# Moving the last GLU weight conversions into the GLU's first pass, with another split order in the main slots

## The chip, the cores and the metric

The kernel runs on one core of a Trainium2 chip. The metric is the device time of one execution in microseconds (us). The kernel before takes 869.46 us (median of three runs, 868.57 to 869.98).

## The reference, cut to what matters

```python
state = f[:, :, t, :, None] * state + k_t (outer) v_t      # linear attention, 4 x 8 heads, 768 steps of 48
y[:, :, t] = q_t @ state
logits = x @ w_gate + modality_bias[modality_id]           # x: y as 3072 tokens of 384
e_idx = argmax(logits); gate_w = softmax(logits)[e_idx]    # one of 8 experts for each token
out[e] = gate_w * (relu(x @ w1[e]) @ w2[e])                # 384 -> 1024 -> 384
gate = 1 / (1 + exp(-(x @ w_gate)))                        # GLU: 384 -> 1536 -> 384
out = (gate * (x @ w_val)) @ w_out
```

The inputs of the GLU's weights reach the chip as 64-bit floats; every other large input is fp32, and the result is fp32.

## The kernel before, in words

**Stages.** Linear attention runs over 24 tiles of 128 tokens, 26 loop iterations with the ends of its pipeline, and ends at about 155 us. Two early expert tiles (`slot32`) follow, then half-size expert positions to about 223 us, then ten **main slots** p = 11 to 20 (`position`, which calls `slot`), up to about 409 us, and last the **GLU**: six passes `t` over 512 tokens each, with twelve steps `f` in a pass. A step is `glu_in` (gate and value projections of 128 columns) and, one step later, `glu_out`.

**Splits.** A matrix product of fp32 precision is made from three products of two rounded parts. `split` (L391 to L394) makes the parts of a weight piece: ScalarE (ACT) copies the piece into the high part, and VectorE (DVE) or GpSimd (POOL) subtracts that from the piece for the low part.

**Slots.** A main slot has ten places f0 to f9 in its row of products, and at each a table `hooks` says what else is issued there. In `position`, the tuple `at` names the places at which the four weight pieces x = 0, 2, 1, 3 of the next slot are split; x = 1 subtracts on POOL, the others on DVE. A split frees its `raw` buffer, and the load of the piece for the slot after goes out on the SP queue at once. At f7 the next slot's tokens are transposed (`transpose_x`, L408 to L411), and POOL issues the gathers of the tokens after them (L398). The ten hidden chunks h of a slot leave through ACT (`hh`, L667) and DVE (`hl`, L668).

**Conversions.** The GLU's weights are nine pieces of 128 x 1536 values in doubles, converted to fp32 half a piece at a time, so 18 conversions. One conversion is a load of 768 KB (`convert_load`), a mask on ACT (`convert_mask`, L849), two DVE operations (`convert_high`, L855 and L858), two more (`convert_low`, L866 and L869) and a store to the DRAM scratch `wd` (`convert_store`); pieces 3 and 7 stay in SBUF tiles `stage` instead. Four conversions stand in attention, at iterations `CONV`, two in the second `slot32`, seven in slots 12 to 18 at f0 and f1, and five more in the slots of `TWICE`, at f5 and f8. In slot 20 the three pieces of `LAST` (4, 5 and 8), by then in `wd`, are loaded into `raw` buffers, and in GLU steps 0 to 5 `split_last` splits a half of one in each step, with POOL's subtraction. Step 1 also splits piece 7 from `stage`, whole, with POOL's subtraction. Pieces 4 and 5 are wanted by `glu_in` at f = 8 of the first pass, piece 8 by `glu_out` at f = 8.

**The GLU's step.** In `glu_in` a gate tile and a value tile (PSUM, tag `gv`, three buffers) are filled by 18 products each. For each half (256 tokens) ACT makes the sigmoid of the gate (L1659), DVE multiplies it by the value (L1660), ACT copies the product to `gh` (L1661), and DVE subtracts for `gl` (L1662). With three buffers in turn, the value tile of step n takes the buffer that held the gate tile of step n - 1. The engines take their instructions in program order, and the hooks in the table `more` (one list for each step n) come behind the step's multiplications on DVE and copies on ACT:

```python
for n, (t, f, halves) in enumerate(seq):
    glu_in(t, f, halves, 256 if n < len(seq) - 1 else 128)
    for step in more.get(n, ()):
        step()
```

Of the kernel before, what the change touches and what calls it, by code (L numbers as in the profile page):

```python
# [14 lines left out]
I32 = mybir.dt.int32  # L15
# [22 lines left out]
NSLOT = NHALF + NSTAT  # L38
# [2 lines left out]
ORDER = (0, 2, 1, 3)  # L41
ROUTE = ((0, 4), (4, 4), (8, 4), (12, 4), (16, 2), (18, 4), (22, 2))
CUM = len(ROUTE) % 2
CONV = (3, 7, 11, 15)
GROUPED = 17
PUT = (9, 13, 17)
GROUP = (0, 6, 1, 2)
STAGED = (3, 7)
PADS = (320, 160, 352, 96)
LAST = ((4, 0), (5, 2), (8, 1))  # L50
TWICE = (13, 14, 16, 17, 18)
MIN_DECAY = 1e-18
MIN_LOGIT = -43.0
CAP = 1e36
# [8 lines left out]
def kernel(  # L63
# [16 lines left out]
    nc = tc.nc  # L80
# [309 lines left out]
    def split(dst, src, eng=None):  # L390

        hi, lo = dst
        nc.scalar.copy(out=hi, in_=src)
        (eng or nc.vector).tensor_tensor(out=lo, in0=src, in1=hi, op=ALU.subtract)  # L394
# [19 lines left out]
    tabs, hp = {}, {}  # L414
# [399 lines left out]
        return ys  # L814


    todo = [(j, half) for j in (0, 1, 6, 2, 3, 7, 4, 5, 8) for half in range(2)]
    loaded, done = [], []
    stage = {}

    def half_of(t, half):
        return t[:, half * 768:(half + 1) * 768]

    def convert_buffers():

        if "cv" in hp:
            cv = hp["cv"]
            return (
                cv.tile([P, 1536], I32, tag="cvr", name="cvr", bufs=2), cv.tile([P, 768], F32, tag="cvm", name="cvm", bufs=2),
                cv.tile([P, 768], I32, tag="cvt", name="cvt"),  # L830
            )
        n = len(todo) % 2 * 2
        return raw[n].bitcast(I32), raw[n + 1][:, 0:768], raw[n + 1][:, 768:1536].bitcast(I32)

    def convert_load():
        if not todo:
            return
        j, half = todo.pop(0)
        r, m, t = convert_buffers()
        if j in stage:  # L840
            m = half_of(stage[j], half)
        nc.sync.dma_start(out=r, in_=w_glu[j].bitcast(I32)[:, half * 1536:(half + 1) * 1536])
        loaded.append((j, half, r.rearrange("p (n o) -> p n o", o=2), m, t))
# [33 lines left out]
            j, half, m = done.pop(0)  # L877
            nc.sync.dma_start(out=half_of(wd[j], half), in_=m)

    def split_last(n, half):  # L880
        j, x = LAST[n]
        split([half_of(t, half) for t in glu[j]], half_of(raw[x], half), nc.gpsimd)


    hp["p"] = ctx.enter_context(tc.tile_pool(name="hp", bufs=2))
# [629 lines left out]
    def position(p, w, w_next):  # L1515
# [12 lines left out]
            each(hooks, f0=[lambda: part(w[2], 2, 1), lambda: load_group(p + 1, 2)], f1=lambda: split_group(p, 1, w), f2=lambda: split_group(p, 3, w))  # L1528
        if NSLOT - NSTAT < p < NSLOT - 2:
            each(hooks, f0=[convert_mask, convert_high], f1=[convert_low, convert_store, convert_load])  # L1530
        if p in TWICE:
            each(hooks, f5=[convert_mask, convert_high], f8=[convert_low, convert_store])
        if p + 1 in TWICE:
            each(hooks, f8=convert_load)
        if p >= NSLOT - NSTAT:
            at = ((2, 0), (3, 2), (4, 1), (6, 3))
            if p == NSLOT - NSTAT:
                at = ((4, 0), (5, 2), (7, 1), (9, 3))
            if p == NSLOT - 1:
                at = ((0, 0), (1, 2), (2, 1), (3, 3))  # L1540
            for f, x in at:
                each(hooks, **{f"f{f}": lambda x=x: split_group(p + 1, x, w_next, nc.gpsimd if x == 1 else None)})
        if p == NSLOT - 1:
            for f, (j, x) in enumerate(LAST):
                each(hooks, **{f"f{f}": lambda j=j, x=x: nc.sync.dma_start(out=raw[x], in_=wd[j])})
        if p == NSLOT - 2:
            each(hooks, f8=lambda: load_x2(0))
        if p == NSLOT - 1:
# [180 lines left out]
    for j, x in ((7, 2), (5, 3)):  # L1729
        glu[j] = alloc_w(*pools[(NSLOT + 1) % 2], x)  # L1730
    glu[8] = alloc_w(wc, "c", 0)
    more = {
        0: [lambda: split_last(0, 0), lambda: split_last(0, 1)],
        1: [lambda: scatter_y(tabs["dst"][:, NSLOT + 4]), lambda: split(glu[7], stage[7], nc.gpsimd)],
        2: [lambda: split_last(1, 0), lambda: load_x2(1)],
        3: [lambda: split_last(1, 1)],
        4: [lambda: split_last(2, 0)],
        5: [lambda: split_last(2, 1)],
    }
    psum.close()  # L1740
    ps_g = psum.enter_context(tc.tile_pool(name="ps_g", bufs=3, space=PSUM))
# [80 lines left out]
```

## Time and profile before

| what | before |
|---|---|
| median of the runs | 869.46 us |
| the profiled execution | 869.35 us |
| its span | 867.6 us |
| granted TensorE clock, mean | 0.993 |
| matmul engine (PE) busy | 843.4 us, 97% of the span |
| DVE busy | 481.2 us, 55% |
| ACT busy | 389.5 us, 45% |
| POOL busy | 251.1 us, 29% |
| main slots | 223.9 to 409 us |
| GLU | 409 us to the end |

The span is the stretch in which the engines work; the execution's time has 1.75 us around it. Busy shares are over the whole span: PE's 97% says that nearly all time passes beside matmuls, not that each of them runs at its shortest.

### The profile page before, as it was taken

Reading aid. Unit: us, or ns where it says so; the run is one execution under the profiler, and the core shown is the slowest. Engines: PE = TensorE matmul, PEld = TensorE weight load, DVE = VectorE, ACT = ScalarE, POOL = GpSimd, SP = SyncE. Lnnn points to the kernel's source line nnn. Section 1 sums busy time; section 2 is a strip of 40 time slices with the busy share of each in tenths; the row PEclk is TensorE's granted clock in tenths of the full one; section 3 lists DMA queues with packets and bytes.
Section 4 is the critical chain, followed back from the end, with each engine's and each line's share of the span. In section 5 each row is a group of like instructions: output and inputs, shape, how many; then the busy total and the mean of one; then the engine's idle time right before and its main releaser. Section 6 shows DMA issues by size and latency. Waiting matters only on the chain.

```text
span 867.6 us, 15306 instructions
## 1 busy us (share of the span) xinstructions
PE 843.4 (97%) x5802; PEld 762.0 (88%) x5802; DVE 481.2 (55%) x1036; ACT 389.5 (45%) x804; POOL 251.1 (29%) x321
## 2 busy tenths in 40 slices
PE   8999999999999999999999999999999999999995
PEld 6999988778999999999888888888888888888885
DVE  5788897576878979964435234334432523342221
ACT  5868664236766666656433322322232332232222
POOL 4755542125265646655620200020020011002002
PEclk9999999999999999999999999999999999999998
DMA  8677745757989889875111120021012002001000
GB/s 300 199 239 265 257 141 225 264 198 229 349 293 329 298 287 322 330 248 195 56 28 47 46 46 19 1 65 28 19 45 46 19 12 54 10 0 37 1 1 36
DMA packets 52273, 121.15 MB, mean 140 GB/s; under 512 B 21018, under 2 KB 33318, under 8 KB 52192
## 3 DMA queue, kind: packets, MB, share of 16 engines
q1 hardware_dynamic: 47200, 105.10, 36.1%
q0 software_dynamic: 4992, 15.00, 5.0%
q8 instruction: 47, 0.77, 0.4%
q14 instruction: 34, 0.28, 0.1%
HBM read 96.44 MB, written 20.11 MB: 134 GB/s over the span
## 4 chain that ended last, share of the span: by engine, by line
PE 68%; DVE 5%; issue 2%; ACT 1%; POOL 0%; DMA 0%; POOLq 0%; DVEq 0%; ACTq 0%
PE gv L1650 11%; PE gv L1651 11%; PE gv L1649 11%; PE y L740 8%; PE o L1674 6%; PE o L1672 6%; PE o L1673 6%; PE h L664 3%; PE h L661 3%; PE h L662 3%; DVE cvt L855 2%; DVE al L394 1%; DVE hl L668 1%; PE xT L408 0%; DVE bl L394 0%
## 5 line engine op out<-in xcount | busy, mean ns | idle before, releaser
L1660 DVE TENSOR_TENSOR sg<-sg,gv 128x256 f32<-128x256 f32 (+1 forms) x145 | 60.2, 415 | 209.4 <-PE gv L1651 209.4
L1661 ACT CAST gh<-sg 128x256 fp32r<-128x256 f32 (+1 forms) x145 | 58.7, 405 | 191.6 <-DVE sg L1660 191.6
L1680 POOL DMA_INDIRECT out_dram<-raw,tok x24 | 23.6, 984 | 375.6 <-ACT raw L1677 368.1
L1662 DVE TENSOR_TENSOR gl<-sg,gh 128x256 fp32r<-128x256 f32 (+1 forms) x145 | 64.3, 443 | 68.2 <-ACT gh L1661 68.2
L1659 ACT ACTIVATE sg<-gv 128x256 f32<-128x256 f32 (+1 forms) x145 | 55.2, 381 | 94.7 <-PE gv L1651 92.6
L398 POOL DMA_INDIRECT xg<-xd,ids x24 | 36.6, 1525 | 61.6 <-PE xT L408 37.2
L667 ACT ACTIVATE hh<-h 128x256 fp32r<-128x256 f32 x80 | 30.8, 386 | 42.5 <-PE h L664 41.5
L668 DVE SCALAR_TENSOR_TENSOR hl<-h,hh 128x256 fp32r<-128x256 f32 x80 | 33.4, 419 | 21.7 <-ACT hh L667 21.4
L950 POOL TENSOR_TENSOR qT<-kq,g 128x512 f32<-128x512 f32 x19 | 28.6, 1507 | 54.4 <-issue 34.5
L1651 PE MATMUL gv<-oddh,al 128*128 128x512 f32 (+1 forms) x120 | 44.3, 369 | 0.0
L1650 PE MATMUL gv<-oddl,ah 128*128 128x512 f32 (+1 forms) x120 | 44.3, 369 | 0.0
L1649 PE MATMUL gv<-oddh,ah 128*128 128x512 f32 (+1 forms) x120 | 44.1, 367 | 0.0
L1651 PE MATMUL gv<-oddh,bl 128*128 128x512 f32 x108 | 42.5, 394 | 0.0
L1651 PE MATMUL gv<-evenh,bl 128*128 128x512 f32 x108 | 42.5, 393 | 0.0
L1650 PE MATMUL gv<-oddl,bh 128*128 128x512 f32 x108 | 42.4, 393 | 0.0
L1650 PE MATMUL gv<-evenl,bh 128*128 128x512 f32 x108 | 42.4, 393 | 0.0
L1651 PE MATMUL gv<-evenh,al 128*128 128x512 f32 x108 | 42.3, 391 | 0.0
L1650 PE MATMUL gv<-evenl,ah 128*128 128x512 f32 x108 | 42.2, 391 | 0.0
L1649 PE MATMUL gv<-evenh,ah 128*128 128x512 f32 x108 | 42.0, 389 | 0.0
L1649 PE MATMUL gv<-evenh,bh 128*128 128x512 f32 x108 | 42.0, 389 | 0.0
L1649 PE MATMUL gv<-oddh,bh 128*128 128x512 f32 x108 | 42.0, 389 | 0.0
L980 DVE TENSOR_TENSOR am<-a,causal 128x512 f32<-128x512 f32 x48 | 31.7, 682 | 7.9 <-PE a L974 7.9
(365 smaller groups left out, 2490.3 us busy)
## 6 DMA issues: line engine op xcount, KB each, us to landing
raw<-in_w_dram SPq DMA_DIRECT2D x48, 768.0 KB, 6.0
kq<-in_att_kq_dram SPq DMA_DIRECT2D x24, 512.0 KB, 5.4
cvr<-in_w_glu_dram SPq DMA_DIRECT2D x14, 768.0 KB, 7.4
raw<-wd SPq DMA_DIRECT2D x7, 768.0 KB, 5.4
f<-in_att_fv_dram SPq DMA_DIRECT2D x24, 200.0 KB, 4.5
v<-in_att_fv_dram SPq DMA_DIRECT2D x24, 200.0 KB, 4.4
x<-yd SPq DMA_DIRECT2D x12, 386.0 KB, 3.5
xd<-rows SPq DMA_DIRECT2D x5, 772.0 KB, 5.2
```

What stands on the lines that cost most here:

```text
L668: nc.vector.scalar_tensor_tensor(out=hl, in0=ps, scalar=0.0, in1=hh, op0=ALU.max, op1=ALU.subtract)
L740: nc.tensor.matmul(out=ps, lhsT=lhs[:, ts], rhs=rhs[:, fs], start=(g == 0 and part == 0), stop=(g == 7 and part == 2))
L1649: nc.tensor.matmul(out=ps[:, ns], lhsT=hi[:, sl], rhs=xh[:, c, ns], start=(c == 0), stop=False)
L1650: nc.tensor.matmul(out=ps[:, ns], lhsT=hi[:, sl], rhs=xl[:, c, ns], start=False, stop=False)
L1651: nc.tensor.matmul(out=ps[:, ns], lhsT=lo[:, sl], rhs=xh[:, c, ns], start=False, stop=(c == 2))
L1659: nc.scalar.activation(out=sg[:, sl], in_=pss[0][:, to], func=AF.Sigmoid)
L1660: nc.vector.tensor_tensor(out=sg[:, sl], in0=sg[:, sl], in1=pss[1][:, to], op=ALU.mult)
L1661: nc.scalar.copy(out=gh[:, sl], in_=sg[:, sl])
L1662: nc.vector.tensor_tensor(out=gl[:, sl], in0=sg[:, sl], in1=gh[:, sl], op=ALU.subtract)
L1672: nc.tensor.matmul(out=ps, lhsT=gh[:, ts], rhs=hi[:, fs], start=(f == 0), stop=False)
L1673: nc.tensor.matmul(out=ps, lhsT=gh[:, ts], rhs=lo[:, fs], start=False, stop=False)
L1674: nc.tensor.matmul(out=ps, lhsT=gl[:, ts], rhs=hi[:, fs], start=False, stop=(f == 11))
```

## The change

Iteration 15 of attention no longer converts, `TWICE` is gone, and the six halves of pieces 4, 5 and 8 are no longer converted ahead. `load_last` brings their doubles into `raw` buffers (two of them in slot 20, one in step 0, two in step 2, one in step 4, into the `stage` tiles), and `convert_last` in GLU steps 0 to 5 converts one half and splits it, the subtraction on DVE. In the main slots the split of x = 3 moves from f6 to f7, behind the transposes; in slot 11 all four move one or two places ahead.

```diff
@@ -41,14 +41,13 @@
 ORDER = (0, 2, 1, 3)
 ROUTE = ((0, 4), (4, 4), (8, 4), (12, 4), (16, 2), (18, 4), (22, 2))
 CUM = len(ROUTE) % 2
-CONV = (3, 7, 11, 15)
+CONV = (3, 7, 11)
 GROUPED = 17
 PUT = (9, 13, 17)
 GROUP = (0, 6, 1, 2)
 STAGED = (3, 7)
 PADS = (320, 160, 352, 96)
-LAST = ((4, 0), (5, 2), (8, 1))
-TWICE = (13, 14, 16, 17, 18)
+LAST = tuple((j, half) for j in (4, 5, 8) for half in range(2))
 MIN_DECAY = 1e-18
 MIN_LOGIT = -43.0
 CAP = 1e36
@@ -814,7 +813,7 @@
         return ys
 
 
-    todo = [(j, half) for j in (0, 1, 6, 2, 3, 7, 4, 5, 8) for half in range(2)]
+    todo = [(j, half) for j in (0, 1, 6, 2, 3, 7) for half in range(2)]
     loaded, done = [], []
     stage = {}
 
@@ -835,8 +834,9 @@
     def convert_load():
         if not todo:
             return
-        j, half = todo.pop(0)
-        r, m, t = convert_buffers()
+        take_half(*todo.pop(0), *convert_buffers())
+
+    def take_half(j, half, r, m, t):
         if j in stage:
             m = half_of(stage[j], half)
         nc.sync.dma_start(out=r, in_=w_glu[j].bitcast(I32)[:, half * 1536:(half + 1) * 1536])
@@ -877,9 +877,16 @@
             j, half, m = done.pop(0)
             nc.sync.dma_start(out=half_of(wd[j], half), in_=m)
 
-    def split_last(n, half):
-        j, x = LAST[n]
-        split([half_of(t, half) for t in glu[j]], half_of(raw[x], half), nc.gpsimd)
+    def load_last(n):
+        a, b = (raw[0:2], raw[2:4], raw[0:2], [stage[j] for j in STAGED])[n if n < 4 else 2 + n % 2]
+        take_half(*LAST[n], a.bitcast(I32), b[:, 0:768], b[:, 768:1536].bitcast(I32))
+
+    def convert_last():
+        convert_mask()
+        convert_high()
+        convert_low()
+        j, half, m = done.pop(0)
+        split([half_of(t, half) for t in glu[j]], m)
 
 
     hp["p"] = ctx.enter_context(tc.tile_pool(name="hp", bufs=2))
@@ -1528,21 +1535,16 @@
             each(hooks, f0=[lambda: part(w[2], 2, 1), lambda: load_group(p + 1, 2)], f1=lambda: split_group(p, 1, w), f2=lambda: split_group(p, 3, w))
         if NSLOT - NSTAT < p < NSLOT - 2:
             each(hooks, f0=[convert_mask, convert_high], f1=[convert_low, convert_store, convert_load])
-        if p in TWICE:
-            each(hooks, f5=[convert_mask, convert_high], f8=[convert_low, convert_store])
-        if p + 1 in TWICE:
-            each(hooks, f8=convert_load)
         if p >= NSLOT - NSTAT:
-            at = ((2, 0), (3, 2), (4, 1), (6, 3))
+            at = ((2, 0), (3, 2), (4, 1), (7, 3))
             if p == NSLOT - NSTAT:
-                at = ((4, 0), (5, 2), (7, 1), (9, 3))
+                at = ((3, 0), (4, 2), (5, 1), (8, 3))
             if p == NSLOT - 1:
                 at = ((0, 0), (1, 2), (2, 1), (3, 3))
             for f, x in at:
                 each(hooks, **{f"f{f}": lambda x=x: split_group(p + 1, x, w_next, nc.gpsimd if x == 1 else None)})
         if p == NSLOT - 1:
-            for f, (j, x) in enumerate(LAST):
-                each(hooks, **{f"f{f}": lambda j=j, x=x: nc.sync.dma_start(out=raw[x], in_=wd[j])})
+            each(hooks, f4=lambda: load_last(0), f5=lambda: load_last(1))
         if p == NSLOT - 2:
             each(hooks, f8=lambda: load_x2(0))
         if p == NSLOT - 1:
@@ -1730,12 +1732,12 @@
         glu[j] = alloc_w(*pools[(NSLOT + 1) % 2], x)
     glu[8] = alloc_w(wc, "c", 0)
     more = {
-        0: [lambda: split_last(0, 0), lambda: split_last(0, 1)],
-        1: [lambda: scatter_y(tabs["dst"][:, NSLOT + 4]), lambda: split(glu[7], stage[7], nc.gpsimd)],
-        2: [lambda: split_last(1, 0), lambda: load_x2(1)],
-        3: [lambda: split_last(1, 1)],
-        4: [lambda: split_last(2, 0)],
-        5: [lambda: split_last(2, 1)],
+        0: [convert_last, lambda: load_last(2)],
+        1: [lambda: scatter_y(tabs["dst"][:, NSLOT + 4]), lambda: split(glu[7], stage[7], nc.gpsimd), convert_last],
+        2: [convert_last, lambda: load_x2(1), lambda: load_last(3), lambda: load_last(4)],
+        3: [convert_last],
+        4: [convert_last, lambda: load_last(5)],
+        5: [convert_last],
     }
     psum.close()
     ps_g = psum.enter_context(tc.tile_pool(name="ps_g", bufs=3, space=PSUM))
```

DVE in slot 13, one of those with a second conversion. `al_...<-raw_118`, `raw_120` and `raw_121` are the split subtractions of x = 0, 2 and 3, `xtl` the transposes' one. Before:

```order
L394 TENSOR_TENSOR al_4482<-raw_118,ah_4481 128x1536
L668 SCALAR_TENSOR_TENSOR hl<-h,hh 128x256
L394 TENSOR_TENSOR al_4486<-raw_120,ah_4485 128x1536
L668 SCALAR_TENSOR_TENSOR hl<-h,hh 128x256 x2
L855 TENSOR_SCALAR cvt<-cvr 128x768
L858 SCALAR_TENSOR_TENSOR cvt<-cvr,cvt 128x768
L668 SCALAR_TENSOR_TENSOR hl<-h,hh 128x256
L394 TENSOR_TENSOR al_4488<-raw_121,ah_4487 128x1536
L668 SCALAR_TENSOR_TENSOR hl<-h,hh 128x256
L411 TENSOR_TENSOR xtl<-xT,xth 128x3x128 x2
L866 SCALAR_TENSOR_TENSOR cvt<-cvr,cvt 128x768
L869 SCALAR_TENSOR_TENSOR stage_2943<-stage_2943,cvt 128x768
```

And changed (all lines of `split` and of the slots are one less there):

```order
L393 TENSOR_TENSOR al_4471<-raw_118,ah_4470 128x1536
L667 SCALAR_TENSOR_TENSOR hl<-h,hh 128x256
L393 TENSOR_TENSOR al_4475<-raw_120,ah_4474 128x1536
L667 SCALAR_TENSOR_TENSOR hl<-h,hh 128x256 x4
L410 TENSOR_TENSOR xtl<-xT,xth 128x3x128 x2
L393 TENSOR_TENSOR al_4477<-raw_121,ah_4476 128x1536
```

The four operations of the second conversion are gone from between the `hl`, and the subtraction of x = 3 stands behind the transposes.

POOL from the entry of slot 11 to its outputs; `al_...<-raw_119` is the split subtraction of x = 1. Before, and then changed:

```order
L641 COPY cur<-xc 128x4
L647 COPY xc<-xg 128x4
L398 DMA xg<-xd,ids 128x386 x2
L394 TENSOR_TENSOR al_3994<-raw_119,ah_3993 128x1536
L690 COPY ysb<-cur 128x2 x2
```

```order
L640 COPY cur<-xc 128x4
L393 TENSOR_TENSOR al_3987<-raw_119,ah_3986 128x1536
L646 COPY xc<-xg 128x4
L397 DMA xg<-xd,ids 128x386 x2
L689 COPY ysb<-cur 128x2 x2
```

The subtraction moved from behind the gathers to ahead of them and of the copy of `xc`.

DVE in GLU step 0 and at the start of step 1, changed. `sg` is the multiplication, `gl` the subtraction of a half, `raw_118` the doubles and `raw_119` the converted half:

```order
L1662 TENSOR_TENSOR sg<-sg,gv 128x256
L1664 TENSOR_TENSOR gl<-sg,gh 128x256
L1662 TENSOR_TENSOR sg<-sg,gv 128x256
L1664 TENSOR_TENSOR gl<-sg,gh 128x256
L855 TENSOR_SCALAR raw_119<-raw_118 128x768
L858 SCALAR_TENSOR_TENSOR raw_119<-raw_118,raw_119 128x768
L866 SCALAR_TENSOR_TENSOR raw_119<-raw_118,raw_119 128x768
L869 SCALAR_TENSOR_TENSOR raw_119<-raw_119 128x768
L393 TENSOR_TENSOR al_6310<-raw_119,ah_6309 128x768
L1662 TENSOR_TENSOR sg<-sg,gv 128x256
```

Before, the two `sg` and two `gl` of step 1 follow those of step 0 directly; now five operations stand between, and the same five in each of the steps 1 to 5. On ACT, step 1 now reads:

```order
L1663 CAST gh<-sg 128x256
L392 CAST ah_6325<-stage_2937 128x1536
L849 ACTIVATE raw_121<-raw_120 128x768
L392 CAST ah_6309<-raw_121 128x768
L1661 ACTIVATE sg<-gv 128x256
```

The cast of piece 7 (`stage_2937`), for which POOL subtracts, stands ahead of the conversion's mask and cast; the next step's sigmoid stands behind all three. PE's order is as before.

## Rows read from the trace of the kernel before

**Rows 1.** The page's first part: busy time of each engine.
```profile
PE 843.4 (97%) x5802; PEld 762.0 (88%) x5802; DVE 481.2 (55%) x1036; ACT 389.5 (45%) x804; POOL 251.1 (29%) x321
```

**Rows 2.** PE's waits, 104 to 160 us: total, times, longest.
```profile
PE take L346 <- DVE table L339: 0.8, 1, 0.8
PE c L928 <- ACT nl L918: 0.7, 1, 0.7
PE rank L278 <- DVE oh L263: 0.6, 1, 0.6
PE xtok L1057 <- ACT raw L734: 0.3, 1, 0.3
```

**Rows 3.** Timeline of ACT, first `hh` of slots 12, 13, 15, 16, 20: start, duration.
```profile
243.19 0.38 ACT L667 ACTIVATE hh<-h 128x256 fp32r<-128x256 f32 x1
...
264.41 0.38 ACT L667 ACTIVATE hh<-h 128x256 fp32r<-128x256 f32 x1 [0.49 <-PE h L664]
...
301.35 0.38 ACT L667 ACTIVATE hh<-h 128x256 fp32r<-128x256 f32 x1 [0.48 <-DVE stage L869]
...
318.93 0.38 ACT L667 ACTIVATE hh<-h 128x256 fp32r<-128x256 f32 x1 [0.49 <-PE h L664]
...
392.00 0.38 ACT L667 ACTIVATE hh<-h 128x256 fp32r<-128x256 f32 x1 [0.49 <-PE h L664]
```

**Rows 4.** Timeline of POOL and DVE, end of slot 11 and slot 13.
```profile
241.76 3.54 POOL L394 TENSOR_TENSOR al<-raw,ah 128x1536 fp32r<-128x1536 f32 x1
242.29 4.63 DVE L394 TENSOR_TENSOR al<-raw,ah 128x1536 fp32r<-128x1536 f32 x1 [2.12 <-ACT ah L393]
...
272.63 3.65 POOL L394 TENSOR_TENSOR al<-raw,ah 128x1536 fp32r<-128x1536 f32 x1 [6.03 <-ACT ah L393]
273.66 3.03 DVE L855 TENSOR_SCALAR cvt<-cvr 128x768 int32<-128x768 int32 x1
```

**Rows 5.** Windows in slot 12: PE, PEld, DVE, ACT, POOL busy, PEclk, DMA share, GB/s.
```profile
245.20:247.30 2.10, 0.28 (x2) 0.02 (x1) 2.10 (x3) 1.74 (x2) 2.01 (x4) 1.00 0.48 108
248.60:251.90 3.30, 3.30 (x15) 3.30 (x14) 3.27 (x6) 1.72 (x2) 2.02 (x3) 0.50 0.89 292
```

**Rows 6.** Timeline of DVE, the conversion at the start of slot 13.
```profile
265.16 0.55 DVE L855 TENSOR_SCALAR cvt<-cvr 128x768 int32<-128x768 int32 x1
265.75 0.96 DVE L858 SCALAR_TENSOR_TENSOR cvt<-cvr,cvt 128x768 int32<-128x768 int32 x1
...
266.96 0.95 DVE L866 SCALAR_TENSOR_TENSOR cvt<-cvr,cvt 128x768 int32<-128x768 int32 x1
267.94 0.96 DVE L869 SCALAR_TENSOR_TENSOR cvm<-cvm,cvt 128x768 f32<-128x768 f32 x1
```

**Rows 7.** Timeline of DVE and ACT, GLU steps 0, 1, 5 and 7.
```profile
413.38 0.42 DVE L1660 TENSOR_TENSOR sg<-sg,gv 128x256 f32<-128x256 f32 x1 [5.21 <-PE gv L1651]
414.15 0.38 ACT L1659 ACTIVATE sg<-gv 128x256 f32<-128x256 f32 x1
415.51 0.42 DVE L1662 TENSOR_TENSOR gl<-sg,gh 128x256 fp32r<-128x256 f32 x1 [0.47 <-ACT gh L1661]
417.46 0.42 DVE L1660 TENSOR_TENSOR sg<-sg,gv 128x256 f32<-128x256 f32 x1 [1.53 <-PE gv L1651]
...
444.83 0.62 DVE L1615 COPY cut<-x 128x384 uint16<-128x384 uint16 x2
...
454.82 0.42 DVE L1660 TENSOR_TENSOR sg<-sg,gv 128x256 f32<-128x256 f32 x1 [2.60 <-PE gv L1651]
```

**Rows 8.** Timeline of POOL, DVE and ACT, 422 to 428 us.
```profile
422.67 3.51 POOL L394 TENSOR_TENSOR al<-stage,ah 128x1536 fp32r<-128x1536 f32 x1
...
424.59 1.88 DVE L1662 TENSOR_TENSOR gl<-sg,gh 128x256 fp32r<-128x256 f32 x1 [0.47 <-ACT gh L1661]
...
427.14 0.83 ACT L393 CAST ah<-raw 128x768 fp32r<-128x768 f32 x1
```

**Rows 9.** The page's DMA issues: KB each, us to landing.
```profile
raw<-in_w_dram SPq DMA_DIRECT2D x48, 768.0 KB, 6.0
...
cvr<-in_w_glu_dram SPq DMA_DIRECT2D x14, 768.0 KB, 7.4
```

## The prediction, made before the changed kernel was timed

> **What bounds the kernel now.** The page's first part comes first [rows 1]: PE is busy for 97% of the span, DVE for 55%. An average like that says where to look, not what a change is worth, so I went on to the waits of PE and the timelines of the three stages that the change touches, and asked in each whether PE or something else sets the pace.
>
> In attention's last third PE waits four times between 104 and 160 us, 2.4 us in all [rows 2]. Otherwise it works without a break.
>
> In the main slots the distance from one slot's first `hh` to the next one's is the pace [rows 3]. Slot 15 takes 318.93 - 301.35 = 17.58 us. It has one conversion and stands outside `TWICE`. The eight slots 12 to 19 together take 392.00 - 243.19 = 148.81, and slot 12 alone 264.41 - 243.19 = 21.22. So slot 12 loses 3.6 to the pace of 17.58, and the five slots of `TWICE` share the rest.
>
> The causes stand in the timelines [rows 4]. In slot 13 the second conversion's first operation takes 3.03 us where the same one took 0.55 at the slot's start [rows 6]: POOL's subtraction began 1.03 us earlier and ran 3.65. DVE got through when POOL was done. At the end of slot 11 DVE's subtraction of x = 3 takes 4.63 beside a POOL one of 3.54 that began 0.53 earlier. The `hl` that slot 12 needs first stand behind it on DVE, and PE is nearly idle from 245.20 to 247.30; after that the granted clock reads 0.50, the lower of its two levels (1.2 of 2.4 GHz), for 3.3 us [rows 5].
>
> In the GLU, DVE waits for PE [rows 7]: from step 1 to step 7 the first multiplication comes every (454.82 - 417.46) / 6 = 6.23 us, and DVE has gaps ended by PE before it. Here PE sets the pace, and DVE has room.
>
> **Term 1, main slots: -8.2 us.** The second conversion goes, and with it the five stalls behind POOL. In slot 11 POOL's subtraction no longer starts just ahead of DVE's last one. If all eight slots run as slot 15 does, they take 8 x 17.58 = 140.6 instead of 148.8: 3.6 from slot 12 and 4.6 from `TWICE`. Moving x = 3 from f6 to f7 sends its next load out one place later, about a tenth of a slot or 1.8 us; a load takes 6.0 [rows 9] and has most of a slot's 17.58, so I cost it at nothing. Without that cover ACT's copy would wait for the landing, and every `hh` behind it. POOL's subtraction in slot 11 now holds its gathers back by up to 3.5, but what they bring is transposed seven places later. The lower bound is 4.6, if the new order in slot 11 only moves the stall; the upper is 8.2, as nothing here takes a slot below PE's own pace.
>
> **Term 2, attention: -1.3 us.** Iteration 15 loses a conversion, four DVE operations of 0.55 + 0.96 + 0.95 + 0.96 = 3.42 us [rows 6], a mask and two DMAs. Most of it lay beside PE's work. Of PE's waits those for `nl` and for `oh`, 0.7 + 0.6 [rows 2], come right after DVE's conversion in a stretch where DVE is full. I take these two: 1.3. The bounds are nothing and all four waits, 2.4.
>
> **Term 3, the first GLU pass: +12.8 us.** Each of steps 0 to 5 gets a mask on ACT (beside DVE's work) and, on DVE, the four conversion operations and a subtraction. What counts is the loop through DVE. From the first multiplication of a step to the end of its last `gl` are 415.51 + 0.42 - 413.38 = 2.55 us [rows 7]; then 3.42 of conversion, ACT's cast of 0.83 [rows 8], which DVE must await, and a subtraction of a half piece, 0.96 by the same-sized last operation of a conversion [rows 6]. With some 0.05 for the handovers that is 7.8 us. The next step's multiplication stands behind it on DVE, and PE can't run ahead: its value products need the buffer of the earlier gate, free when the second sigmoid has run, 414.15 + 0.38 - 413.38 = 1.15 us into a step. So the pace is 7.8, not 6.23.
>
> In step 1 the whole of piece 7 is split as well. POOL's subtraction takes 3.51, and in the trace DVE's `gl` beside it took 1.88 where it takes 0.42: it ended when POOL did [rows 7, 8]. By the order, POOL's now falls between the operations of a conversion, all of which the rows of slot 13 let me expect to wait. I take the whole 3.5. The bounds are nothing (POOL gets in only in gaps that DVE has anyway) and 3.5.
>
> Counted from step 0's first multiplication, step 6 begins at 6 x 7.8 + 3.5 + 0.6 (the first `cut` copies, [rows 7], stand behind step 5's conversion) = 50.9. Step 6 and later have no conversion, so PE sets the pace again: step 7's value products start 1.2 after step 6 and take half of 4.08 (step 1's whole `glu_in`, 417.46 - 413.38), so its multiplication comes at 50.9 + 1.2 + 2.06 + 0.1 = 54.3. Before it came at 454.82 - 413.38 = 41.44. The difference is 12.8. The low end without POOL's hold is 9.3; the high end adds 1.65 for the clock (below).
>
> The loads have cover. The longest wait from issue is 7.4 [rows 9]. The buffer of step 0's conversion is free some 5 us into that step, so its next doubles land by 12.4 and are converted in step 2, which begins at 19.1; those of step 4 are issued about 24 and land by 32, and step 4 begins at 34.7. The DMAs removed (stores and loads through `wd`) free transfers that nothing waited for: zero.
>
> **The sum** is -8.2 - 1.3 + 12.8 = +3.3. The profiled execution took 869.35, so 872.65, or 872.7. The median of the runs is 0.1 above that execution, which changes nothing.
>
> **The clock.** After the 2.1 us gap in slot 12 the lower level of the clock held for 3.3 us [rows 5]; at half speed that costs 3.3 x 0.5 = 1.65 us. In the first GLU pass PE will stand about 1.5 us in each of five steps and 5 us around step 2. If the clock fell after each, the work of a step would take 6.23 + 1.65 = 7.9, about DVE's own 7.8, so it would be mostly hidden; only the last one shows. The Trainium skill, "TensorE: Matmul & The Clock Gate", section "HAM oscillation — how this bites in real kernels", says that a matmul engine which stands waiting between bursts is throttled again and pays at half rate after each. The row of slot 12 agrees for one gap. By that rule the sum would be the second case below.
>
> **The rivals.**
> *Clock falls with the stalls*: as just said, 12.8 + 1.65, in all +5.0, so 874.3. For it speaks the row of slot 12; against it, that the stalls of 1.5 are shorter than that gap.
> *POOL's hold costs nothing* (the side of "not slower"): in step 1 POOL subtracts in the time in which DVE awaits the cast, or after the conversion. Then term 3 is 9.3 against gains of 9.5: -0.2, so 869.2. It decides if POOL gets through in steps 1 and 2 without lengthening a DVE operation. Against it stand the two rows in which DVE waited for POOL's end.
> *Attention gives all its waits*: -2.4 in place of -1.3, so 871.6.
> *Slot 11 keeps its stall*: if a piece of slot 12 lands too late for its new place (6.0 us a load [rows 9], with the places moved up by two), ACT's copy waits, POOL's subtraction starts late and again meets DVE's. 3.6 of the gain is gone: 876.3.
> *Gains larger and hold gone*: 9.3 - 8.2 - 2.4 = -1.3, and with a conversion's loop overlapping the next step by some tenths in each of six steps (7.4 in place of 7.8 is 2.4) about 866.
> *The change doesn't take the second conversions out*: the order of DVE shows them gone, so none is left for this.
>
> **How the numbers follow.** A measurement of this kernel tells about 0.2% from no change, 1.7 us. The forecast has 0.41, the clock 0.20, POOL's hold gone 0.13, attention's waits 0.10, slot 11's stall 0.06, and the last case 0.10. The last is faster: 0.10. POOL's case lies within 0.2%, and of the forecast and of attention's case some low part (0.05) falls there too: 0.18. The rest is slower: 0.72. The range takes in POOL's case with a little below it and reaches up to slot 11's: 868.0 to 876.5. It leaves out the last case and what lies above.
>
> **What would show it.** First `hh` of slots 12 to 20 every 17.6 us, also in slot 12; no `L855` of 3 us there. Multiplications of GLU steps 0 to 6 at distances of 7.8 with one of about 11.3, PE waiting for the sigmoid (`gv`) in each; step 7 some 54 us after step 0; one conversion operation in step 1 of over 3 us beside POOL. In attention the two waits shortened. The prediction is wrong if the first GLU pass keeps 6.2 us a step (then about 860), or if a slot takes over 18 us.

## The result and the profile after

The changed kernel takes 873.49 us (median of five runs, 872.83 to 876.15), the kernel before 869.46 beside it (five runs, 867.46 to 869.98). The medians differ by 4.0 us. The ratio, which takes in every run, is 1.0057, with a 95% interval of 1.0037 to 1.0076, which is 3.2 to 6.6 us: slower. The forecast was 872.7, slower by 3.3. The profiled execution of the changed kernel is its longest, 876.15 us with a span of 874.5; before it was 867.6. So the traces differ by 6.9 us, the medians by 4.0, and the account below has to say where that surplus lies.

First the page's busy times, which answer to [rows 1]. Then two views of PE's waits (total, times, longest). The first is the main slots of the kernel before, 243 to 392 us; for those of the changed one, 243 to 384, the view lists none. The second is the first GLU pass of the changed kernel, 405 to 460.

```profile
PE 845.7 (97%) x5802; PEld 763.8 (87%) x5802; DVE 475.1 (54%) x1042; ACT 390.3 (45%) x804; POOL 235.7 (27%) x315
```

```profile
PE y L740 <- DVE hl L668: 4.9, 6, 1.8
```

```profile
PE gv L1651 <- ACT sg L1661: 8.6, 4, 4.5
```

PE is 97% busy in both, so the page tells nothing of the change. The waits do: six waits of PE for `hl` in the slots are gone, and in the GLU's first pass PE now waits for the second sigmoid of a step, once for 4.5 us.

**Main slots.** The timeline of ACT, first `hh` of slots 12, 13 and 20, answering to [rows 3]:

```profile
243.50 0.38 ACT L666 ACTIVATE hh<-h 128x256 fp32r<-128x256 f32 x1 [0.49 <-PE h L663]
...
261.07 0.38 ACT L666 ACTIVATE hh<-h 128x256 fp32r<-128x256 f32 x1 [0.49 <-PE h L663]
...
384.16 0.38 ACT L666 ACTIVATE hh<-h 128x256 fp32r<-128x256 f32 x1 [0.49 <-PE h L663]
```

Slot 12 takes 17.57 and the eight slots 140.66, where they took 148.81: 8.15 us less, and each of them is at PE's pace. Of the 8.15 the view lists 4.9 as waits; 1.5 more is the lower clock behind slot 12's wait (run 7), and the rest stands in no listed wait. (A slot has eight hidden chunks, and not the ten of the description ahead: from one first `hh` to the next there are eight.)

**First GLU pass.** The timeline of DVE: the first multiplications of steps 0, 1, 2, 6, 7 and 8, with one operation of step 1's conversion, answering to [rows 7]; then POOL beside it, answering to [rows 8].

```profile
405.57 0.42 DVE L1662 TENSOR_TENSOR sg<-sg,gv 128x256 f32<-128x256 f32 x1 [5.21 <-PE gv L1653]
...
413.49 0.41 DVE L1662 TENSOR_TENSOR sg<-sg,gv 128x256 f32<-128x256 f32 x1
...
417.52 4.17 DVE L866 SCALAR_TENSOR_TENSOR raw<-raw,raw 128x768 int32<-128x768 int32 x1
...
424.55 0.41 DVE L1662 TENSOR_TENSOR sg<-sg,gv 128x256 f32<-128x256 f32 x1
...
456.44 0.41 DVE L1662 TENSOR_TENSOR sg<-sg,gv 128x256 f32<-128x256 f32 x1
...
460.71 0.42 DVE L1662 TENSOR_TENSOR sg<-sg,gv 128x256 f32<-128x256 f32 x1 [0.60 <-PE gv L1653]
...
467.85 0.42 DVE L1662 TENSOR_TENSOR sg<-sg,gv 128x256 f32<-128x256 f32 x1 [1.95 <-PE gv L1653]
```

```profile
417.03 3.83 POOL L393 TENSOR_TENSOR al<-stage,ah 128x1536 fp32r<-128x1536 f32 x1 [9.54 <-ACT ah L392]
```

Step 1 begins 7.92 us after step 0, step 2 another 11.06 later, and steps 3 to 5 follow at 7.84. The rows of steps 1 to 6 no longer end in a wait for PE (`[... <-PE gv ...]`): DVE is never idle before these multiplications, it is late. In step 1 DVE's third conversion operation began 0.49 after POOL's subtraction and ended 0.83 after it.

Two windows of the changed kernel's first pass (columns as in [rows 5]) show the lower clock behind PE's longest wait, of 4.5 us, and behind its last one, of 1.8:

```profile
427.00:430.00 3.00, 3.00 (x8) 2.32 (x8) 2.83 (x5) 0.45 (x1) 0.00 (x0) 0.50 0.00 0
460.00:463.00 3.00, 3.00 (x12) 2.90 (x11) 1.46 (x5) 1.09 (x3) 0.00 (x0) 0.58 0.65 127
```

**Start and attention.** The same state update of DVE (`ss`) early in attention, and the first early expert output (`ysb` on ACT) after it, before and then changed:

```profile
35.64 0.34 DVE L1002 TENSOR_TENSOR ss<-ss,u 128x192 f32<-128x192 f32 x1
...
178.10 0.58 ACT L724 ACTIVATE ysb<-y,cur 128x384 f32<-128x384 f32 x1 [2.14 <-PE y L699]
```

```profile
36.98 0.34 DVE L1009 TENSOR_TENSOR ss<-ss,u 128x192 f32<-128x192 f32 x1
...
177.61 0.58 ACT L723 ACTIVATE ysb<-y,cur 128x384 f32<-128x384 f32 x1 [2.14 <-PE y L698]
```

Between the two lie 142.46 us before and 140.63 after: attention gave 1.83. But the changed execution was already 1.34 late at the first of them, where no instruction differs.

**Into slot 11.** ACT's first `hh` of slot 11 in the changed kernel, behind a cast that waited 1.12 us for a weight piece's load; before, that cast did not wait:

```profile
225.68 0.84 ACT L1479 CAST bh<-raw 128x768 fp32r<-128x768 f32 x1 [1.12 <-DMA raw<-in_w_dram]
226.42 0.38 ACT L666 ACTIVATE hh<-h 128x256 fp32r<-128x256 f32 x1
```

The account of the two profiled executions, each row worked out as the difference of the same distance in both traces. In the kernel before, step 8 begins at 461.05:

```profile
461.05 0.42 DVE L1660 TENSOR_TENSOR sg<-sg,gv 128x256 f32<-128x256 f32 x1 [0.94 <-PE gv L1651]
```

| stretch | before | after | difference |
|---|---|---|---|
| start to the `ss` above | 35.64 | 36.98 | +1.34 |
| to the first early output | 142.46 | 140.63 | -1.83 |
| to slot 11's first `hh` | 47.79 | 48.81 | +1.02 |
| slot 11 | 17.30 | 17.08 | -0.22 |
| slots 12 to 19 | 148.81 | 140.66 | -8.15 |
| slot 20 to the first multiplication | 21.38 | 21.41 | +0.03 |
| GLU steps 0 to 7, to step 8's first multiplication | 47.67 | 62.28 | +14.61 |
| the rest | 406.55 | 406.65 | +0.10 |

Together +6.9; the last row lies within the rounding of the spans, which are given to a tenth. Over all traces here the stretch from the early output to slot 11 varied from 47.6 to 48.8 without order, and the start by 4 us; both are left out of the comparison of the kernels. The surplus of 2.9 over the medians is as large as the start's 1.34 and the clock's second fall, 1.55 (run 3), together. That these two are what the other executions lacked is likely and not shown: the other four have a mean granted clock of 0.990 and the profiled one 0.987, and the profiled execution of run 1, whose trace has no second fall, has 0.990 too.

### The profile page after: what moved, and what is told of

Same layout as the page of the kernel before. It is cut to its first block, busy times and chain, and to the rows that moved or that the text cites. A ratio compares the mean times of both kernels' runs of the same rounds, so it can differ in the third digit from the quotient of the medians.

```text
span 874.5 us, 15277 instructions
## 1 busy us (share of the span) xinstructions
PE 845.7 (97%) x5802; PEld 763.8 (87%) x5802; DVE 475.1 (54%) x1042; ACT 390.3 (45%) x804; POOL 235.7 (27%) x315
## 4 chain that ended last, share of the span: by engine, by line
PE 67%; DVE 4%; ACT 2%; issue 1%; DMA 1%; POOL 0%; DVEq 0%; POOLq 0%; ACTq 0%
PE gv L1653 10%; PE gv L1652 10%; PE gv L1651 10%; PE y L739 10%; PE o L1676 5%; PE o L1674 5%; PE o L1675 5%; PE h L660 3%; PE h L663 3%; PE h L661 3%; DVE raw L866 1%; DMA raw<-in_w_dram 1%; PE xT L407 1%; ACT gh L1663 1%; DVE sg L1662 1%
## 5 line engine op out<-in xcount | busy, mean ns | idle before, releaser
L1664 DVE TENSOR_TENSOR gl<-sg,gh 128x256 fp32r<-128x256 f32 (+1 forms) x145 | 61.5, 424 | 68.2 <-ACT gh L1663 68.2
L397 POOL DMA_INDIRECT xg<-xd,ids x24 | 28.6, 1190 | 52.6 <-PE xT L407 27.6
L392 ACT CAST ah<-raw 128x1536 fp32r<-128x1536 f32 (+1 forms) x23 | 32.1, 1396 | 14.4 <-DVE raw L869 11.4
```

The costliest lines, as they stand in the source:

```text
L1664: nc.vector.tensor_tensor(out=gl[:, sl], in0=sg[:, sl], in1=gh[:, sl], op=ALU.subtract)
```

## The experiments

Where a run is split into stretches, the start before the `ss` row is left out for the reason told at the end.

**1. Piece 7 subtracted on DVE.**

```diff
-lambda: split(glu[7], stage[7], nc.gpsimd), convert_last]
+lambda: split(glu[7], stage[7]), convert_last]
```

> The changed kernel, with piece 7's subtraction in GLU step 1 on DVE instead of POOL. My theory: POOL's hold lies on the path. In the changed kernel's trace one conversion operation of step 1 took 4.17 us where the others took 0.96, 3.2 more; on DVE the same subtraction takes 1.75. Step 1 gets 1.5 shorter, PE's wait behind it falls from 4.5 to about 3, and with it may go some of the time at the lower clock that follows: 872.0, or about 871 with the clock. Rival (POOL's hold costs nothing, DVE would have waited anyway): the 1.75 comes on top, 875.2.

Measured: 872.99 us (nine runs), ratio to before 1.0041 (1.0026 to 1.0056). Step 1 shrinks from 11.06 to 10.55 only. DVE's timeline in step 1:

```profile
416.24 1.76 DVE L393 TENSOR_TENSOR al<-stage,ah 128x1536 fp32r<-128x1536 f32 x1 [0.96 <-ACT ah L392]
```

The rival is out: the time did not rise by 1.75. But my number was wrong as well. DVE paid 0.96 for ACT's cast and 1.76 for the subtraction, 2.7 in place of the 3.2 of POOL's hold; PE's wait behind it fell to 4.0, not to 3. The test mixed two costs, so the hold was measured by itself in run 9.

**2. The new order of the splits alone, in the kernel before.**

```diff
-            at = ((2, 0), (3, 2), (4, 1), (6, 3))
+            at = ((2, 0), (3, 2), (4, 1), (7, 3))
             if p == NSLOT - NSTAT:
-                at = ((4, 0), (5, 2), (7, 1), (9, 3))
+                at = ((3, 0), (4, 2), (5, 1), (8, 3))
```

> The kernel before, with the new places of the splits in the main slots (x = 3 at f7; in slot 11 f3, f4, f5, f8) and nothing else. My theory: slot 12's 3.6 us came from the order in slot 11, where POOL's subtraction began just ahead of DVE's last one: 865.9, slot 12 at about 17.6 us and the slots with a second conversion still at about 18.5, each with a first conversion operation of 3 us. Rival: slot 12's stall comes from its own conversion or from late pieces, and the order changes nothing: 869.5. Other rival: x = 3 at f7 collides with the second conversion's last operations and the slots get longer: over 870.

Measured: 861.03 us (six runs), ratio 0.9916 (0.9895 to 0.9938). The theory and both rivals missed: it is 8.7 us below the 869.69 measured beside it, with all five second conversions still in the slots. The `hh` of slots 12, 13, 14 and 20, then DVE in slot 13:

```profile
242.10 0.38 ACT L667 ACTIVATE hh<-h 128x256 fp32r<-128x256 f32 x1 [0.48 <-PE h L664]
...
259.69 0.38 ACT L667 ACTIVATE hh<-h 128x256 fp32r<-128x256 f32 x1 [0.49 <-PE h L664]
...
277.26 0.39 ACT L667 ACTIVATE hh<-h 128x256 fp32r<-128x256 f32 x1 [0.48 <-PE h L664]
...
383.56 0.38 ACT L667 ACTIVATE hh<-h 128x256 fp32r<-128x256 f32 x1 [0.49 <-PE h L664]
```

```profile
268.95 3.08 DVE L855 TENSOR_SCALAR cvt<-cvr 128x768 int32<-128x768 int32 x1
272.06 0.96 DVE L858 SCALAR_TENSOR_TENSOR cvt<-cvr,cvt 128x768 int32<-128x768 int32 x1
272.94 0.75 DVE L668 SCALAR_TENSOR_TENSOR hl<-h,hh 128x256 fp32r<-128x256 f32 x2
273.60 1.01 DVE L411 TENSOR_TENSOR xtl<-xT,xth 128x384 fp32r<-128x384 f32 x2
275.02 1.76 DVE L394 TENSOR_TENSOR al<-raw,ah 128x1536 fp32r<-128x1536 f32 x1 [0.40 <-ACT ah L393]
```

The conversion still stands 3.08 us behind POOL, as before [rows 4]. Yet slot 13 takes 17.57 and the eight slots 141.46, and the view of PE's waits lists none in them. What changed is who stands behind it. In the kernel before the same stretch read:

```profile
276.73 0.96 DVE L858 SCALAR_TENSOR_TENSOR cvt<-cvr,cvt 128x768 int32<-128x768 int32 x1
277.61 0.42 DVE L668 SCALAR_TENSOR_TENSOR hl<-h,hh 128x256 fp32r<-128x256 f32 x1
277.94 1.75 DVE L394 TENSOR_TENSOR al<-raw,ah 128x1536 fp32r<-128x1536 f32 x1
279.61 0.41 DVE L668 SCALAR_TENSOR_TENSOR hl<-h,hh 128x256 fp32r<-128x256 f32 x1
279.94 1.01 DVE L411 TENSOR_TENSOR xtl<-xT,xth 128x384 fp32r<-128x384 f32 x2
```

There the subtraction of x = 3, which nobody wants before the next slot, stood between two `hl`, for the last of which PE waited 0.6 us. At f7 both `hl` and the tokens (`xtl`) pass ahead of it, and the stall of 3 us finds room.

**3. Attention's conversion put back.**

```diff
-CONV = (3, 7, 11)
+CONV = (3, 7, 11, 15)
```

> The changed kernel with a conversion at iteration 15 of attention again (four of its twelve there, and none left for slot 18). My theory: the conversion at 15 costs what the traces show from iteration 6 to the first early expert output, 142.46 us in the kernel before and 140.63 in the changed one: 1.8 longer, 875.3. Rival (the prediction's term, the two waits): 874.8 at most, and hardly to be told from that. Other rival: attention's DVE has room and the difference comes from the start of the execution, 873.5.

Measured: 877.35 us (six runs), ratio 1.0089 (1.0067 to 1.0110). From `ss` to the early output it takes 142.51 us, against 140.63: 1.88, as the first theory says. The conversion that slot 18 loses by this edit was free there: the eight slots take 140.66 as without it. The total rose by 3.9, twice that, and so no theory has the median; where its other 2 us lie was not shown. In the profiled execution the start is late, 38.45 us to `ss`, but the medians hold executions of which no trace was kept. The stretch decides, and the median has the right sign.

This run also shows the first pass with the clock up behind the last wait: steps 6, 7 and 8 begin at 50.85, 54.50 and 60.73 after step 0, where the profile of the changed kernel has 50.87, 55.14 and 62.28. So the pass costs 60.73 - 47.67 = 13.06 us without the clock's fall, and 1.55 more with it.

**4. No conversions in the first pass.**

```diff
     def convert_last():
-        convert_mask()
-        convert_high()
-        convert_low()
-        j, half, m = done.pop(0)
+        j, half, r, m, t = loaded.pop(0)
         split([half_of(t, half) for t in glu[j]], m)
```

> The changed kernel without the six conversions in GLU steps 0 to 5 (mask and four DVE operations each left out, so three weight pieces hold no weights); their loads and their splits stay. My theory: the DVE loop falls from 7.8 us to 2.55 + 0.83 + 0.96 = 4.35 a step, less than PE's 6.23, so PE sets the pace again and the whole loss of the pass is gone, in the trace of the changed kernel 13.7 us up to step 7 and 0.9 more at a lower clock behind it: 859 to 861. Rival: a part of the loss comes from the loads of doubles or from the splits on DVE, which stay: over 864.

Measured: 860.44 us (six runs), ratio 0.9905 (0.9884 to 0.9926). Step 8 begins 47.67 after step 0, exactly as before. So the loads and the splits cost nothing, and the conversions with their place are the whole of the loss. One step was late: a split's subtraction took 3.63 us beside POOL's 3.50 of piece 7, step 2 began at 11.87 in place of 10.31, and step 3 came on time again. So POOL's hold, 3.2 us on the path of the changed kernel (run 9), cost nothing where the steps behind it had room.

**5. The same conversions spread over ten steps.**

```diff
+        0: [high_last, convert_low, lambda: load_last(2)],
+        1: [lambda: scatter_y(tabs["dst"][:, NSLOT + 4]), cast_last, high_last, sub_last],
+        2: [convert_low, high_last, lambda: load_x2(1), lambda: load_last(3)],
+        3: [cast_last, convert_low, sub_last, cast_seven, lambda: load_last(4)],
+        4: [cast_last, sub_seven, sub_last],
+        5: [high_last, convert_low, lambda: load_last(5)],
+        6: [cast_last, high_last, sub_last],
+        7: [convert_low, high_last],
+        8: [cast_last, convert_low, sub_last],
+        9: [cast_last, sub_last],
```

(What is taken out, and the functions themselves, are left out here. `high_last` is a conversion's mask and first two DVE operations, `cast_last` the ACT cast of a converted half, `sub_last` its DVE subtraction, `cast_seven` and `sub_seven` the same for piece 7. The cuts and joins stand at steps 7 to 10.)

> The changed kernel with the same work in another order in the first pass: the conversions cut into halves and spread over steps 0 to 9, each half's ACT cast and DVE subtraction one step after its conversion so that DVE never waits for the cast, piece 7's subtraction on DVE in step 4, and the preparation of the next pass's tokens two steps later. My theory: DVE has 6.23 - 2.55 = 3.7 us of room in a step; six conversions with their subtractions take 6 x 4.4 and piece 7 1.75, 28 us, which fits into ten steps, and PE keeps 6.2 a step: the loss of the pass is gone, 859 to 861, faster than both kernels. Rival: anything behind a step's multiplications delays the next ones, wherever it stands, and the pass still loses most of it: over 866.

Measured: 861.83 us (six runs), ratio 0.9914 (0.9893 to 0.9936). The loss of the pass is gone but for about 1 us: steps 4 to 7 begin 22.76, 28.99, 35.22 and 41.44 after step 0, as before. Step 10, with three joins for the next pass, took 8.78.

**6. The joins spread as well.**

```diff
-    first = {7: ((cut_x2, 0),), 8: ((cut_x2, 1), (cut_x2, 2)), 9: ((cut_x2, 3), (join_x2, 0))}
-    first[10] = ((join_x2, 1), (join_x2, 2), (join_x2, 3))
+    first = {6: ((cut_x2, 0),), 7: ((cut_x2, 1),), 8: ((cut_x2, 2), (cut_x2, 3))}
+    first.update({9: ((join_x2, 0), (join_x2, 1)), 10: ((join_x2, 2), (join_x2, 3))})
```

> The spread conversions as in the run before, with the preparation of the next pass's tokens divided otherwise: cuts in steps 6, 7 and 8 (two), joins two each in steps 9 and 10. My theory: in the spread run the step with three joins took 8.8 us instead of 6.2, which cost 1.0 us behind it, and the conversions themselves cost nothing more: 1.0 less than the spread run, about 860.5, as much as without conversions. Rival: the conversions cost the difference and it stays at 861.8.

Measured: 860.74 us (six runs), ratio 0.9898 (0.9877 to 0.9920). Step 12 begins 73.03 us after step 0, against 72.58 in the kernel before and 73.59 in run 5. So 0.56 of the expected 1.0 came back, and 0.45 is left of the pass's loss; the medians of the two runs differ by 1.1, less than their width. DVE's first multiplications of steps 0, 9, 10, 11 and 12:

```profile
405.04 0.42 DVE L1675 TENSOR_TENSOR sg<-sg,gv 128x256 f32<-128x256 f32 x1 [5.21 <-PE gv L1666]
...
459.07 0.41 DVE L1675 TENSOR_TENSOR sg<-sg,gv 128x256 f32<-128x256 f32 x1
...
467.02 0.41 DVE L1675 TENSOR_TENSOR sg<-sg,gv 128x256 f32<-128x256 f32 x1
...
473.68 0.42 DVE L1675 TENSOR_TENSOR sg<-sg,gv 128x256 f32<-128x256 f32 x1
...
478.07 0.42 DVE L1675 TENSOR_TENSOR sg<-sg,gv 128x256 f32<-128x256 f32 x1 [1.85 <-PE gv L1666]
```

Steps 9 and 10 are 1.7 and 0.4 too long and step 11 comes back by 1.8: a delay of two us in DVE alone was nearly made good by the step behind it, which had room.

**7. x = 3 at f7 alone, in the kernel before.**

```diff
-            at = ((2, 0), (3, 2), (4, 1), (6, 3))
+            at = ((2, 0), (3, 2), (4, 1), (7, 3))
```

> The kernel before with x = 3 split at f7 in slots 12 to 19 and nothing else. Theory after the run with the new order alone: two parts of the order each remove a stall, this one those of the slots with a second conversion (0.9 each becomes about 0.2, 3.8 in all), while slot 12 keeps its 21.2 us: 865.7. Rival: the places in slot 11 do it all, by giving the later slots their pieces sooner: 869, slots 13, 14, 16, 17 and 18 at 18.5.

Measured: 865.37 us (twelve runs), ratio 0.9959 (0.9946 to 0.9971), 4.2 faster: the first theory. Slot 13 takes 17.57 and slots 13 to 19 together 388.10 - 264.21 = 123.89, in the kernel before 127.59: 3.7 for this one place. Slot 12 keeps a stall, 19.71 here and not the 21.2 expected. The first `hh` of slots 13 and 20:

```profile
264.21 0.38 ACT L667 ACTIVATE hh<-h 128x256 fp32r<-128x256 f32 x1 [0.48 <-PE h L664]
...
388.10 0.38 ACT L667 ACTIVATE hh<-h 128x256 fp32r<-128x256 f32 x1 [0.48 <-PE h L664]
```

**8. The second conversions' DVE work left out, old order.**

```diff
-            each(hooks, f5=[convert_mask, convert_high], f8=[convert_low, convert_store])
+            each(hooks, f5=convert_mask, f8=[skip_low, convert_store])
```

> The kernel before in its old order, with the four DVE operations of each second conversion (slots 13, 14, 16, 17, 18) left out, so that five half pieces hold no weights; loads, masks and stores stay. The prediction's account: the second conversions cost 4.6 us in the old order: 864.9, these slots at 17.6 us, slot 12 still at 21.2. Rival: the old order stalls beside POOL's subtraction whatever is converted: 869.5.

Measured: 863.81 us (six runs), ratio 0.9933 (0.9912 to 0.9955). Slots 13 to 19 take 387.68 - 264.60 = 123.08, which is 4.5 less than before. So the prediction's 4.6 was right for the old order. Slot 12 took 19.87, not the 21.2 expected. With run 7, either remedy alone removes the stall or most of it: taking out the second conversion (4.5), or taking the split from in front of the `hl` (3.7). They don't add. The first `hh` of slots 13 and 20:

```profile
264.60 0.38 ACT L667 ACTIVATE hh<-h 128x256 fp32r<-128x256 f32 x1 [0.49 <-PE h L664]
...
387.68 0.38 ACT L667 ACTIVATE hh<-h 128x256 fp32r<-128x256 f32 x1 [0.49 <-PE h L664]
```

**9. No POOL subtraction in step 1.**

```diff
-        0: [convert_last, lambda: load_last(2)],
+        0: [convert_mask, lambda: nc.scalar.copy(out=glu[7][0], in_=stage[7]), rest_last, lambda: load_last(2)],
...
-lambda: split(glu[7], stage[7], nc.gpsimd), convert_last]
+convert_mask, lambda: nc.scalar.copy(out=glu[7][1], in_=stage[7]), rest_last]
```

> The changed kernel without POOL's subtraction of piece 7 in GLU step 1: its low part is an ACT copy instead (so it is not a low part), in time in which ACT has nothing else, and its high part's cast stands in step 0. My theory: POOL's hold put 3.2 us on the path in step 1 (one conversion operation of 4.17 in place of 0.96). Without it the distance from step 1's first multiplication to step 2's falls from 11.06 to 7.84, and nothing else changes: about 870.3, unless the clock does otherwise. The run with the subtraction on DVE gained only 0.5 in that distance because DVE there waited 0.96 for ACT's cast and then took 1.76 itself. Rival: DVE is held up there by something else too, and the distance stays over 10: 873.5.

Measured: 869.43 us (twelve runs), ratio 0.9996 (0.9978 to 1.0015). DVE's timeline from step 1's first multiplication to step 2's:

```profile
414.20 0.42 DVE L1665 TENSOR_TENSOR sg<-sg,gv 128x256 f32<-128x256 f32 x1
...
418.24 0.96 DVE L866 SCALAR_TENSOR_TENSOR raw<-raw,raw 128x768 int32<-128x768 int32 x1
...
422.03 0.41 DVE L1665 TENSOR_TENSOR sg<-sg,gv 128x256 f32<-128x256 f32 x1
```

Step 1 takes 7.83, the operation 0.96. Step 8 begins 59.06 us after step 0, in the changed kernel's profile 62.28, both with the lower clock behind the last wait (granted clock 0.57 from 456 to 460 here): the hold of POOL is 3.2 us of the loss, the whole of it on the path. In the median the run is 4.1 below the changed kernel; what of the other 0.9 is start and what is clock was not separated.

**10. The new places in slot 11 alone, in the kernel before.**

```diff
-                at = ((4, 0), (5, 2), (7, 1), (9, 3))
+                at = ((3, 0), (4, 2), (5, 1), (8, 3))
```

> The kernel before with the new places of the splits in slot 11 and nothing else. My theory: slot 12 falls to 17.6 us, the slots with a second conversion stay at 18.5. The stall in slot 12 is 2.1 us by itself (19.7 where the clock stays up, as in two runs of the old order) and 3.6 where the lower clock follows (21.2, as in the profile of before): 865.9 if the clock fell in most executions of the kernel before, 867.4 if not. Rival: this part of the order does nothing by itself, and slot 12 stalls on its own conversion: 869.5.

Measured: 866.57 us (eleven runs), ratio 0.9958 (0.9941 to 0.9975). Slot 12 takes 259.54 - 241.97 = 17.57, slots 13 and 14 18.47 and 18.49. The median lies between the two values that I gave, so the clock's part in the runs of before stays open; the stall itself is this order's. Slots 13 and 14 kept theirs, as the theory said. In the trace of run 7 slot 12 has PE idle too, and the clock at full rate behind it, unlike [rows 5]:

```profile
246.00:248.00 2.00, 0.80 (x7) 0.54 (x5) 2.00 (x1) 1.34 (x2) 2.00 (x2) 1.00 0.33 49
248.00:250.00 2.00, 1.37 (x9) 1.37 (x10) 1.97 (x5) 0.40 (x1) 1.82 (x5) 1.00 0.84 332
250.00:252.00 2.00, 2.00 (x17) 2.00 (x16) 1.97 (x4) 1.11 (x2) 1.83 (x2) 1.00 0.98 286
```

**11. New order, and attention's conversion moved to slot 15.**

```diff
-CONV = (3, 7, 11, 15)
+CONV = (3, 7, 11)
...
-TWICE = (13, 14, 16, 17, 18)
+TWICE = (13, 14, 15, 16, 17, 18)
```

(on top of the edit of run 2)

> The kernel before with the new order in the main slots, and attention's conversion at iteration 15 moved to slot 15 as a second one (six slots with two conversions, none in the GLU). My theory: attention gives its 1.8 us, and a second conversion in the new order costs its slot 0 to 0.4: 861.0 - 1.8 + 0.2 = 859.4, below the order alone. Rival: three slots in a row with two conversions leave DVE no time to catch up, the stall of 0.9 returns in each of the six and takes the gain back: 861 or more.

Measured: 860.98 us (six runs), ratio 0.9886 (0.9864 to 0.9907). In the trace attention gives its 1.9 (from `ss` to the early output 140.64) and the eight slots take 142.16, 0.7 more than in run 2: six second conversions cost 142.16 - 140.66 = 1.5 in all. So the stages came out near the theory, 0.25 to 0.3 for a second conversion and not the rival's 0.9, though the median is the rival's. From `ss` to the end of the span it is about 823.5 us, in run 2 824.8, in run 6 822.5, in the kernel before 832.0. The medians of the three, 860.7 to 861.0, can't be told apart. Each beats the kernel before by 1% and the changed one by 1.4%.

## Why the prediction was right

**The sum.** +3.3 was forecast, +4.0 measured in the medians. As the traces have them, the three terms make +3.1 without the clock's second fall in the pass and +4.6 with it: -8.15 - 1.83 + 13.06 or 14.61. The steps named were the right ones; how they made up the slots' gain was partly wrong, as follows.

**Term 1, -8.2.** The slots gave 8.15, all at PE's pace. The size was right, and so were the five stalls behind POOL: without the second conversions' work the old order loses its 4.5 (run 8). What was wrong is that I costed "Moving x = 3 from f6 to f7" at nothing, because I looked only at the load that it sends out later. In the kernel before it is worth 3.7 by itself (run 7), and with the new order in place the second conversions cost only 141.46 - 140.66 = 0.8 (run 2 against the changed kernel). A slot lost its 0.9 only with both, the conversion held up by POOL and the subtraction of x = 3 between the two `hl`; I saw the first alone. That did not spoil the sum, since both were undone, but it hid that the order alone gives 7.35 of the slots' 8.15, and moving the conversions into the GLU all of the loss. The 3.6 for slot 11's order is shown in run 10; of these 2.1 are the stall and 1.5 the clock, which stays up in other executions (runs 7 and 8, slot 12 at 19.71 and 19.87). I didn't split them: against an execution of the kernel before in which the clock stays up, term 1 would be 6.6, so that part of the close fit is luck.

**Term 2, -1.3.** Measured 1.83 in the changed kernel and 1.88 the other way in run 3. The two waits taken were too few; the bounds, nothing and 2.4, held it. PE's wait for `nl` is gone and the one for `oh` is 0.4 in place of 0.6, so the two waits taken gave 0.9 of the 1.8. PE's busy time between the two rows fell as well, from 138.28 to 137.47 us with as many matmuls (their ends are modelled); why they took less time is not shown. So the mechanism forecast holds for half of this term.

**Term 3, +12.8.** Measured 13.06 without the clock's fall (run 3) and 14.61 in the profile with it. The pace of 7.8 was 7.84, POOL's hold 3.2 (run 9) in place of 3.5, step 7 at 54.5 (run 3) in place of 54.3. Run 4 shows that the loads cost nothing, as was said, though the reason given was too short: the 7.4 of [rows 9] is a median and not the longest wait. In the trace no first operation of a conversion waits for its doubles.

**The rivals.** *Clock falls with the stalls*: in the profile it fell behind the 4.5 us wait, where it was hidden as reckoned, and behind the last wait, of 1.8 us, where it cost 1.55, reckoned as 1.65. The second fall is in run 9's trace too. In runs 1 and 3 the same last wait, of 1.8 us, went by without it, so this rival is right for some executions and not for others. Behind the waits of 1.3 us (reckoned as 1.5) the clock did not fall. The waits of the changed kernel from 445 to 460 us are one of these and the last one, and two windows around the first of them have the clock up:

```profile
PE gv L1651 <- ACT sg L1661: 3.2, 2, 1.8
```

```profile
448.00:451.00 3.00, 1.75 (x8) 1.45 (x9) 2.06 (x6) 1.91 (x4) 0.00 (x0) 1.00 0.03 5
451.00:454.00 3.00, 3.00 (x17) 2.84 (x16) 2.83 (x4) 0.00 (x0) 0.00 (x0) 1.00 0.00 0
```

The rule of the Trainium skill, "TensorE: Matmul & The Clock Gate", section "HAM oscillation — how this bites in real kernels", names bursts of matmuls with waits between that throttle again each time. Here that agrees with the 4.5 us wait, not with those of 1.3, and with that of 1.8 in two traces out of four.

*POOL's hold costs nothing*: out, by run 9. *Attention gives all its waits*: out as a mechanism, since the waits for `table` and for `raw` stand at 0.8 and 0.3 as before; the 1.83 lies halfway between my 1.3 and its 2.4, and neither size is shown. *Slot 11 keeps its stall*: out, slot 12 takes 17.57. *Gains larger and hold gone*: out, with a step of 7.84 and a hold of 3.2.

## What to carry to other kernels

Before a stalled operation is removed, read what stands behind it on its engine: moving work that nobody awaits behind the results that the next engine wants cost nothing here and gave 3.7 of the 4.5 that removing the operation gave. And work moved to an engine that is "half idle" must be set against the idle time of each step of the loop. Six conversions cost 13 us, 3.2 of it POOL's hold, when each had to fit whole into one step. Cut into pieces over ten steps, with the cast and the subtraction a step behind the conversion and piece 7's subtraction on DVE, they cost 0.45.

## What the runs showed of the hardware that was not expected

The first 20 us differ from execution to execution. The granted clock of the window from 10 to 20 us is 0.83 in the profile of before, 0.66 in that of the changed kernel and 1.00 in run 2, though the engines' instructions up to the `ss` row are the same in all three; the `ss` row comes at 35.64, 36.98 and 34.36. The three windows, in this order:

```profile
10.00:20.00 10.00, 8.60 (x105) 7.72 (x107) 6.59 (x13) 4.73 (x9) 2.57 (x9) 0.83 0.97 329
```

```profile
10.00:20.00 10.00, 7.88 (x80) 6.70 (x80) 5.96 (x11) 4.18 (x8) 3.19 (x11) 0.66 1.04 359
```

```profile
10.00:20.00 10.00, 8.33 (x128) 7.51 (x129) 7.39 (x15) 5.78 (x12) 2.76 (x10) 1.00 1.01 347
```

Over the thirteen traces here `ss` came between 34.36 and 38.59, and it follows this clock: 34.36 to 34.70 in the four traces with 1.00 in that window, 35.64 with 0.83, 36.50 to 37.25 in the six with 0.66, and 38.45 and 38.59 in the two with 0.61 and 0.62. PE's wait for `nl` in this stretch does not order them: it is 2.1 us in the changed kernel's profile and 1.4 in the two latest ones. The four us between the earliest and the latest are as much as the change itself, so the stretches from a fixed event on were worth more than the totals. Whether the lower clock alone makes `ss` late, and why the clock falls in some executions, was not tried.
